# Four attention layers on one core: which exponentials VectorE takes over, chosen while the work is laid out instead of by a fixed table

## The chip, the cores and the metric

The kernel runs on one core of one Trainium2 chip. The metric is the time of one execution in microseconds on the device. Three executions of the kernel before took 2187.83, 2191.64 and 2196.76 us, a median of 2191.64 us. A further execution was taken by the profiler, and all rows below come from it.

The engines are named as in the profile: PE (TensorE, matrix products; PEld its weight loads), ACT (ScalarE, here nearly only exponentials), DVE (VectorE, elementwise work), POOL (GpSimd, masks and the issuing of some transfers), SP (SyncE, the issuing of the other transfers). SBUF is the on-chip memory, PSUM the accumulator that PE writes, eight banks of 512 numbers in each of 128 partitions.

## The reference

Two attention blocks A and B with their own weights are applied in turn, A, B, A, B, each to the layer-normed residual stream. S = 2048 tokens, D = 640, 32 heads of 20 numbers. A looks back over a window of 256 tokens, B looks at all tokens.

```python
qkv = (x @ wqkv).reshape(B, S, 3, H, Dh)...          # q, k, v per head
scores = jnp.einsum("bhqd,bhkd->bhqk", q, k) * (Dh ** -0.5)
# A only: scores = where(0 <= i - j < 256, scores, -1e9)
p = softmax(scores, axis=-1)
o = jnp.einsum("bhqk,bhkd->bhqd", p, v)
return o.reshape(B, S, D) @ wo

x = x + A(layernorm(x)); x = x + B(layernorm(x))
x = x + A(layernorm(x)); x = x + B(layernorm(x))
```

In B every one of 32 heads has 2048 x 2048 scores, and each of them goes through an exponential. That is the bulk of the work.

## The kernel before

Layers are numbered 0 to 3; 0 and 2 are windowed (A), 1 and 3 are full (B). Queries are cut into four chunks c of 512, heads into eight groups g of four. A *unit* is a layer, a chunk and a head group; in layers 1 and 3 chunk 0 is further cut by keys into parts, so that it can start before all keys exist. A full unit has 16 blocks of 128 keys times 4 heads, 64 *banks* of scores (128 keys by 512 queries each, one PSUM bank). The list `units` fixes their order: chunk 0 of layer 0, then the rest of layer 0 with three parts of layer 1's chunk 0 between, then layer 1 from chunk 1 with layer 2 woven in after some of its head groups, then layer 3.

**The main loop** takes one *tile* of scores per turn: three banks (two in every second turn of the early units, and a fourth now and then in layer 3's last chunks), which stand in one half of PSUM, banks 0 to 2 and 3 to 5 in turn. PE writes the scores, ACT takes the exponential of the whole tile in one instruction into an SBUF tile `pt` (line 1387), and two or three turns later PE multiplies values by it (line 1420) and accumulates the unit's output in PSUM bank 7. After a unit's last block `finish_unit` copies that bank out with DVE. Everything is written out in program order; each engine runs its own instructions in that order, and semaphores hold it where data or a buffer is missing.

**Background work** (layer norms, projections, output projections, the division by the row sums in `t_tail`) is a set of Python generators. In each turn `background` pumps some of them, with a credit set by `rate` from how much work is due before which unit. They use PSUM banks 5 and 6, one after the other, and DVE empties those banks (`evac`, lines 307 to 331). `keep_clock` adds matmuls of constants (`masks,ident`) where PE would otherwise have less to do than a set amount.

**Banks aside.** Some banks are not given to ACT. DVE computes their exponential in fp16 bit arithmetic, two banks (a *pair*) at a time. The scores of each bank are converted to fixed point (line 957), then follows a chain of four steps on the pair of 1024 columns: the fraction (line 969), its square (978), a cubic (980), and the sum with the whole part (982). The result is multiplied with the values by two matmuls of line 1010. The pair needs an input buffer `xi`, a shared scratch `t` and an output buffer `out`. In layer 1 these live in the space of `raw_o` (two inputs, three outputs), in layer 3 in idle transposed-input tiles and idle key and query tiles (two inputs, five outputs), set up by `side_early` and `side_start`.

Which banks these are is a fixed table: `put_aside` gives each full unit from chunk 1 on the last blocks of its keys, 4 banks in layer 1 and 8 or 6 in turn in layer 3, with none in layer 3's first chunk (nor in chunk 1's first head group). All tiles up to layer 3's chunk 1 are put together before the loop starts: in layer 1 a bank aside stands as the third bank of a tile (ACT then takes only two) at every fifth tile of the unit. In layer 3 from chunk 1 on the bank goes to PSUM bank 6 beside a full tile, when `side_free` finds a loaded unit, a free bank and a free input.

**The planner's backlog** `state["lag"]` estimates how far DVE is behind, in us: each DVE instruction adds a set cost, each turn takes off the time that ACT needs for its tile. The chain is advanced by `side_work` at the end of a turn:

```python
while (force or state["lag"] < WORK) and side["chain"]:   # WORK = 1.0
    cost = next(side["chain"][0], None)
```

At a unit's last block `side_done` forces whatever of its pairs is still missing.

The functions around the change follow with the line numbers of the profile.

Of the kernel before, what the change touches and what calls it, by code (L numbers as in the profile page):

```python
# [23 lines left out]
NT = S // P  # L24
# [16 lines left out]
WORK = 1.0  # L41
SIDE_1 = 4
SIDE_3 = (6, 8)
# [9 lines left out]
def kernel(  # L53
# [629 lines left out]
    def put_aside(l, c, g):  # L683

        if l == 1:
            n = SIDE_1
        else:
            n = 4 if (c, g) == (NC - 1, G - 1) else SIDE_3[g % 2]
        if n == 2:
            return ((NT - 1, 2), (NT - 1, 3))  # L690
        return tuple((NT - 1 - i // 4, i % 4) for i in range(n))

# [3 lines left out]
    class Unit:  # L696
        def __init__(self, l, c, g, part=None):
            self.l, self.c, self.g, self.part = l, c, g, part
            self.windowed = l % 2 == 0
            self.aside = ()  # L700
            if self.windowed:
                sets = [(m, b0, subs, j) for m, b0, subs in window_banks(c) for j in range(4)]
            else:

                if c > 0 and (l, c, g) != (3, 1, 0):
                    self.aside = put_aside(l, c, g)
                k0, k1 = key_blocks(l, part)
                sets = [
                    (None, 0, [(kc, 0, 4, 0)], j) for kc in range(k0, k1) for j in range(4)
                    if (kc, j) not in self.aside  # L710
                ]
            n = len(sets)
            self.banks = [
                (self, j, m, b0, subs, i < 4, i >= n - 4 + len(self.aside), i == n - 1)
                for i, (m, b0, subs, j) in enumerate(sets)
            ]
# [144 lines left out]
    def finish_unit(u):  # L861
# [31 lines left out]
    side_todo = deque(  # L893
        (u, p, i) for u in units for p in range(len(u.aside) // 2) for i in range(2)
    )
    side_left = Counter({id(u): len(u.aside) for u in units})
    side_out = {}
    side = {"xi": deque(), "chain": deque(), "out": deque(), "late": False}
# [7 lines left out]
    def side_start():  # L906

        assert live["xnT"] == 0 and not side["chain"] 
# [28 lines left out]
    def side_scores():  # L937

        u, p, i = side_todo[0]
        mseq[0] += 1  # L940
        mfree[6] = (state["tick"] + 2, mseq[0])
        kc, j = u.aside[2 * p + i]
        z = ps[:, 6, :]
        nc.tensor.matmul(z, lhsT=u.k(kc, j), rhs=u.q(j, 0, 4), start=True, stop=True)  # L944
        side_fixed(z)

    def side_fixed(z):

        u, p, i = side_todo.popleft()
        side_left[id(u)] -= 1  # L950
        if not side_left[id(u)] and id(u) in deferred:
            live["kt"] -= 1
            live["qt"] -= 1
        if i == 0:
            side["now"] = side["xi"].popleft()
        xi = side["now"]
        nc.vector.tensor_scalar(  # L957
# [4 lines left out]
        if i == 1:  # L962
            side["chain"].append(t_chain(u, xi))

    def t_chain(u, xi):
# [3 lines left out]
        V.tensor_scalar(  # L969
            out=t, in0=xi.bitcast(I16)[:, 0::2], scalar1=T1, scalar2=T0, op0=ALU.mult, op1=ALU.add  # L970
        )
        yield 0.7
        while not side["out"]:
            yield 0.0
        pt = side["out"].popleft()
        po = pt.rearrange("p a b -> p (a b)")
        q = po.bitcast(F16)
        V.tensor_tensor(out=q, in0=t, in1=t, op=ALU.mult)  # L978
        yield 0.7
        V.scalar_tensor_tensor(out=q, in0=q, scalar=TB, in1=t, op0=ALU.add, op1=ALU.mult)  # L980
        yield 1.2
        V.scalar_tensor_tensor(
            out=po.bitcast(U16), in0=xi.bitcast(I32), scalar=1.0 / C, in1=q,
            op0=ALU.mult, op1=ALU.add,
        )
        side["xi"].append(xi)
        side_out.setdefault(id(u), []).append((pt, state["tick"]))
        yield 1.2

    def side_work(force):  # L990

        while (force or state["lag"] < WORK) and side["chain"]:
            cost = next(side["chain"][0], None)
            if cost is None:
                side["chain"].popleft()
                continue
            if cost == 0.0:
                return False
# [5 lines left out]
    def side_values(u, pairs, done):  # L1004

        for n in range(done, len(pairs)):
            pt = pairs[n][0]
            for i in range(2):
                kc, j = u.aside[2 * n + i]
                nc.tensor.matmul(  # L1010
                    op[32 * j : 32 * j + VW, :], lhsT=u.v(kc, j), rhs=pt[:, i, :], start=False,
                    stop=all(jj != j for _, jj in u.aside[2 * n + i + 1 :]),
                    skip_group_check=True,
                )
            side["out"].append(pt)

    def side_push():
# [3 lines left out]
        if side_free():  # L1021
            side_scores()
# [7 lines left out]
    def side_done(u):  # L1030

        n = 0
        while len(side_out.get(id(u), ())) < len(u.aside) // 2:
            n += 1
            assert n < 10000
            side_push()
        return side_out.pop(id(u))
# [5 lines left out]

    def s_emitted(u):
# [6 lines left out]
        elif side_left[id(u)]:  # L1051
# [187 lines left out]
    with tc.manual_schedule():  # L1239
# [11 lines left out]
        banks = [b for u in units for b in u.banks]  # L1251
        tiles = []
        starts = {}
        n = 0
        last_layer = sum(len(u.banks) for u in units[: index[3, 1, 0, None]])
        placed = {}
        while n < last_layer:
            size = 2 if len(tiles) % 2 and narrow(banks[n][0]) else 3
            u = banks[n][0]
            at = placed.setdefault(id(u), [])  # L1260
            extra = []
            if (
                len(at) < len(u.aside) and banks[n + 1][0] is u
                and len(tiles) >= (15 // (SIDE_1 - 1) if SIDE_1 > 2 else 3) * len(at) + (at or [0])[0]
            ):
                kc, j = u.aside[len(at)]
                extra = [(u, j, "side", 0, [(kc, 0, 4, 0)], False, False, False)]
                at.append(len(tiles))
                size = 2
            for b in banks[n : n + size]:  # L1270
                starts.setdefault(id(b[0]), len(tiles))
            tiles.append(banks[n : n + size] + extra)
            n += size
        for m, b in enumerate(banks[n:]):
            starts.setdefault(id(b[0]), len(tiles) + m // 3)
        banks = deque(banks[n:])

        side_now = False

        def next_tile(t):  # L1280

            if t < len(tiles):
                return tiles[t]
            size = 3
            if side_now:
                return [banks.popleft() for _ in range(min(size, len(banks)))]
# [236 lines left out]
```

## Time and profile before

| | before |
|---|---|
| median of three executions | 2191.64 us |
| lowest, highest | 2187.83, 2196.76 us |
| profiled execution, its own time | 2197.81 us |
| its span, first to last instruction | 2196.1 us |
| ACT busy | 2112.9 us (96%) |
| PE busy | 1931.1 us (88%) |
| DVE busy | 1324.3 us (60%) |
| POOL busy | 483.3 us (22%) |
| granted PE clock, mean | 0.993 |

The page also gives the busy share in 40 equal slices of the span (one slice is 54.9 us), a digit for tenths. The groups name a line of the kernel, engine, operation, what it writes and reads, how many there were, the busy time, the mean length of one, and the engine's idle time just before them with what ended it. In the tables of stretches each engine has its busy time and, in brackets, its number of instructions. Records of consecutive ACT instructions overlap a little, so sums of lengths can pass the length of a stretch.

### The profile page before, as it was taken

The numbers are of one execution on the slowest core, as the hardware profiler recorded it, in microseconds if no ns is written. First come the engines' busy times: TensorE is split into PE (matmuls) and PEld (weight loads), VectorE is DVE, ScalarE is ACT, GpSimd is POOL, SyncE is SP. The second block draws the span as 40 slices with busy tenths as digits, with TensorE's granted clock in tenths as the row PEclk, the third lists the DMA queues.
The fourth block names the chain that finished last, engine by engine and source line by source line (L and its number), as shares of the span: only waits on it lengthen the run. The fifth ranks groups of instructions, "written<-read, shape, count | busy, mean of one in ns | idle before, by whom it ended". The sixth has DMA issues, their size and how long they took to land. (4 is left out here: it accounts for less than half of the span.)

```text
span 2196.1 us, 73000 instructions
## 1 busy us (share of the span) xinstructions
PE 1931.1 (88%) x31782; PEld 760.4 (35%) x31783; DVE 1324.3 (60%) x2308; ACT 2112.9 (96%) x1726; POOL 483.3 (22%) x952
## 2 busy tenths in 40 slices
PE   8999998988889888888888988888888988888887
PEld 3444443433333333333333433342222222222222
DVE  5556565425656666566665743532487778778873
ACT  7789899999999999999999999999999999999997
POOL 6665556110121113401143112511000000000000
PEclk9899999999999999999999999999999999999999
DMA  6223233322210323112231123122112111111100
GB/s 201 74 82 107 68 98 99 81 78 64 74 46 27 83 60 90 39 37 64 64 101 34 35 86 98 39 57 65 48 43 61 32 32 41 35 32 35 53 20 17
DMA packets 88416, 137.27 MB, mean 63 GB/s; under 512 B 20766, under 2 KB 63486, under 8 KB 88094
## 3 DMA queue, kind: packets, MB, share of 16 engines
q1 hardware_dynamic: 68878, 79.43, 13.1%
q0 software_dynamic: 19216, 53.17, 8.2%
q8 instruction: 249, 4.08, 0.8%
q14 instruction: 73, 0.60, 0.1%
HBM read 99.52 MB, written 27.79 MB: 58 GB/s over the span
## 5 line engine op out<-in xcount | busy, mean ns | idle before, releaser
L1387 ACT ACTIVATE pt<-ps 128x1536 bf16<-128x1536 f32 (+2 forms) x1646 | 2072.1, 1438 | 46.1 <-PE ps L1359 36.1
L1359 PE MATMUL ps<-qt,kt 32*128 32x512 bf16 x3938 | 542.4, 384 | 79.3 <-ACT pt L1387 70.2
L307 PE MATMUL ps<-masks,ident 128*32 128x512 bf16 x5676 | 504.6, 387 | 99.4 <-ACT pt L1387 54.8
L1420 PE MATMUL ps<-pt,vt 128*21 128x512 bf16 x3826 | 383.1, 387 | 1.1 <-issue 1.1
L1359 PEld LDWEIGHTS <-kt 32*128 32x128 bf16 x3938 | 161.0, 91 | 482.7 <-issue 461.0
L307 PEld LDWEIGHTS <-ident 128*32 128x32 bf16 x5676 | 179.9, 94 | 283.1 <-issue 254.7
L1463 POOL TENSOR_SCALAR_AFFINE_SELECT pt<-pt 128x256 bf16<-128x256 bf16 (+2 forms) x505 | 213.2, 444 | 184.4 <-ACT pt L1387 181.8
L307 PE MATMUL ps<-xnT,wqk 128*32 128x512 bf16 x3320 | 224.8, 381 | 12.4 <-DVE on L1128 2.8
L331 DVE CAST st<-ps 128x512 bf16<-128x512 f32 x134 | 92.7, 691 | 169.1 <-PE ps L307 164.9
L1420 PEld LDWEIGHTS <-vt 128*21 128x21 bf16 x3842 | 95.0, 89 | 254.9 <-issue 251.5
L957 DVE TENSOR_SCALAR xnT<-ps 128x512 int32<-128x512 f32 x158 | 109.2, 691 | 109.2 <-PE ps L944 108.4
L307 PE MATMUL ps<-wop,on 128*32 128x320 bf16 x3712 | 160.9, 300 | 6.8 <-DVE x_sb L579 3.3
L1474 DVE TENSOR_TENSOR pt<-pt,masks 128x512 bf16<-128x512 bf16 (+4 forms) x267 | 111.3, 433 | 61.3 <-ACT pt L1387 59.8
L307 PEld LDWEIGHTS <-on 128*32 128x32 bf16 x5760 | 122.2, 95 | 66.6 <-issue 33.6
L1359 PE MATMUL ps<-qa,ka 32*128 32x384 bf16 (+2 forms) x1408 | 114.5, 278 | 24.4 <-ACT pt L1387 21.2
L307 PE MATMUL ps<-wv,xnT 128*32 128x320 bf16 x2560 | 116.6, 302 | 7.9 <-DVE on L1128 3.3
L579 DVE TENSOR_TENSOR x_sb<-x_sb,ps 128x320 bf16<-128x320 bf16 x120 | 58.3, 486 | 105.8 <-PE ps L307 104.9
L307 PEld LDWEIGHTS <-wqk 128*32 128x32 bf16 x3320 | 83.5, 96 | 95.9 <-issue 38.0
L1128 DVE TENSOR_TENSOR on<-on,ps 128x512 bf16<-128x512 bf16 x128 | 86.3, 683 | 47.8 <-PE ps L307 46.9
L885 DVE CAST on<-ps 128x512 bf16<-128x512 f32 x112 | 77.1, 688 | 61.7 <-PE ps L1010 36.1
L957 DVE TENSOR_SCALAR raw_o<-ps 128x512 int32<-128x512 f32 x96 | 66.1, 689 | 61.4 <-PE ps L1359 60.3
L546 POOL DMA_DIRECT2D k_d<-st x75 | 42.6, 568 | 224.2 <-DVE st L331 209.1
(101 smaller groups left out, 1638.5 us busy)
## 6 DMA issues: line engine op xcount, KB each, us to landing
vt<-v_d SPq DMA_DIRECT2D x48, 336.0 KB
kt<-k_d SPq DMA_DIRECT2D x192, 80.0 KB
wqk<-in_B_wqkv_dram POOLq DMA_DIRECT2D x80, 160.0 KB, 3.5
wqk<-in_A_wqkv_dram POOLq DMA_DIRECT2D x70, 160.0 KB, 3.5
k_d<-st POOLq DMA_DIRECT2D x75, 128.0 KB, 2.3
q_d<-st POOLq DMA_DIRECT2D x75, 128.0 KB, 2.1
qt<-q_d SPq DMA_DIRECT2D x384, 20.0 KB
v_d<-vs POOLq DMA_DIRECT2D x16, 336.0 KB, 3.1
```

The costliest lines, as they stand in the source:

```text
L307: nc.tensor.matmul(out_[r], lhsT=lhsT[:, r], rhs=rhs, start=start, stop=stop)
L331: nc.vector.tensor_copy(out=out_, in_=in_)
L546: nc.gpsimd.dma_start(out=dst, in_=staging.pop())
L579: nc.vector.tensor_tensor(out=xv, in0=had, in1=yp, op=ALU.add)
L885: nc.vector.tensor_copy(out=oT, in_=op)
L957: nc.vector.tensor_scalar(out=xi.bitcast(I32)[:, i * C : (i + 1) * C], in0=z, scalar1=SCALE * LOG2E * FIX, scalar2=127.5 * FIX, op0=ALU.mu ...
L1128: nc.vector.tensor_tensor(out=oT, in0=oT, in1=zb, op=ALU.mult)
L1359: nc.tensor.matmul(sp[:, i, col * P : (col + qn) * P], lhsT=u.k(kc, j), rhs=u.q(j, q0, qn), start=True, stop=True,)
L1387: nc.scalar.activation(out=pt[:, i:k, b0 * P :], in_=sp[:, i:k, b0 * P :], func=ACT.Exp, scale=SCALE,)
L1420: nc.tensor.matmul(op[32 * j : 32 * j + VW, q0 * P : (q0 + qn) * P], lhsT=u.v(kc, j), rhs=pg[:, i, col * P : (col + qn) * P], start=(first ...
L1463: nc.gpsimd.affine_select(out=v, in_=v, compare_op=ALU.is_gt if later else ALU.is_ge, fill=0.0, base=0, pattern=[[0, k - i], [-1 if later ...
L1474: nc.vector.tensor_tensor(out=pt_[:, i:k, cols], in0=pt_[:, i:k, cols], in1=mv_, op=ALU.mult)
```

## The change

The table `put_aside`, the tile list that was made ahead, and the counters that went with them are gone. Each unit now keeps a queue `rest` of its banks, and tiles are taken from it turn by turn. In every turn, while the backlog is under 0.5, `side_giver` looks for a unit, the current one or one of the next two, that is loaded and has enough banks left (30, or 12 when nothing has been taken from it by a tile), and `side_take` takes two banks from the end of its queue as the next pair.

Up to layer 3's chunk 1 a bank aside is still the third bank of a three-bank tile, and until `side_start` has run two of them are at least five turns apart (`GAP_1`). `side_start` now runs in layer 3's chunk 0, from its fifth head group on, as soon as at most one transposed-input tile is in use, so that this chunk gives banks too. From chunk 1 on the bank goes to PSUM bank 6 as before. A chain step is now issued only if the backlog with the step's own cost stays under 1.7 (`WORK_1`, until `side_start`) or 2.2 (`WORK`, from then on). A pair's values are multiplied as soon as the pair has been done for three turns. Some of the planner's costs change, and `rate` works from fractions of units instead of numbers of tiles.

In the built program VectorE has 300 banks instead of 254. The numbers of transfers on SP are the same, 1481.

```diff
 LAG = 0.5
-WORK = 1.0
-SIDE_1 = 4
-SIDE_3 = (6, 8)
+LAG_1 = 0.5
+WORK = 2.2
+WORK_1 = 1.7
+KEEP = 30
+HALF = False
+MOST_1 = 64
+GAP_1 = 5
...
-            state["lag"] += 0.6
+            state["lag"] += 0.7 if in_.shape[-1] == C else 0.5
...
-        state["lag"] += 1.2
+        state["lag"] += 1.1
...
+        def pop(self):
+            if self.windowed:
+                return self.rest.popleft()
+            kc, j = self.rest.popleft()
+            end = not self.rest
+            return (self, j, None, 0, [(kc, 0, 4, 0)], kc == self.k0, end, end)
...
-    def side_free():
-        if not side_todo or not side["late"]:
-            return False
-        u, p, i = side_todo[0]
-        return (
-            id(u) in loaded and state["tick"] >= loaded[id(u)] + 8
-            and mfree[6][0] <= state["tick"] and (i == 1 or len(side["xi"]) > 0)
-        )
+    def side_giver():
+        if not side["late"] and state["tick"] < side["last"] + GAP_1:
+            return None
+        if side["half"] is not None:
+            return side["half"][0]
+        if not side["xi"]:
+            return None
+        while side["at"] < len(givers) and not givers[side["at"]].rest:
+            side["at"] += 1
+        for n in range(side["at"], min(side["at"] + 3, len(givers))):
+            u = givers[n]
+            if id(u) not in loaded or state["tick"] < loaded[id(u)] + 8:
+                return None
+            if not side["late" if u.l == 3 else "early"]:
+                return None
+            if u.l == 1 and len(u.aside) >= MOST_1:
+                continue
+            if len(u.rest) >= (KEEP if len(u.rest) + len(u.aside) < u.size else 12):
+                side["at"] = n
+                return u
+        return None
+
+    def side_take(u):
+        if side["half"] is not None:
+            return side["half"][1]
+        j = u.rest.pop()
+        i = u.rest.pop()
+        u.aside += (i, j)
+        side["half"] = (u, i, j)
+        return i
...
     def side_work(force):
-        while (force or state["lag"] < WORK) and side["chain"]:
-            cost = next(side["chain"][0], None)
...
+        while side["chain"]:
+            step, h, cost = side["chain"][0][0]
+            if step.__name__ == "square" and not side["out"]:
+                return False
+            if not force and state["lag"] + cost > (WORK if side["late"] else WORK_1):
+                return False
...
+        def next_tile(t, giver):
+            if state["unit"] < final:
+                size = 2 if t % 2 and narrow(flow[0]) else 3
+                if giver is None or size == 2:
+                    return take(size)
+                kc, j = side_take(giver)
+                return take(2) + [(giver, j, "side", 0, [(kc, 0, 4, 0)], False, False, False)]
...
-                if t >= len(tiles) and not side["late"] and not live["xnT"] and not todo:
+                if (
+                    not side["late"] and state["unit"] >= index[3, 0, 4, PARTS[3][0]]
+                    and live["xnT"] <= 1 and not live["qa"] and not live["ka"]
+                ):
                     side_start()
-                side_now = (
-                    state["held"] is None and state["lag"] < LAG and side_free()
-                )
-                cur = next_tile(t)
+                giver = side_giver() if state["lag"] < (LAG if side["late"] else LAG_1) else None
+                if giver is not None and state["unit"] >= final and (
+                    state["held"] is not None or mfree[6][0] > state["tick"]
+                ):
+                    giver = None
+                cur = next_tile(t, giver)
```

`final` is the first unit of layer 3's chunk 1. The steps of the chain are the same four, now kept as a list of functions instead of a generator (`HALF` is off, so they stay undivided).

More of the change, by code (lines that the diff above doesn't have):

```diff
@@ L891 @@
     ended_units = []
-    side_todo = deque(
-        (u, p, i) for u in units for p in range(len(u.aside) // 2) for i in range(2)
-    )
-    side_left = Counter({id(u): len(u.aside) for u in units})
     side_out = {}
-    side = {"xi": deque(), "chain": deque(), "out": deque(), "late": False}
+    side = {
+        "xi": deque(), "chain": deque(), "out": deque(), "late": False, "early": False,
+        "half": None, "at": 0, "last": 0,
+    }
+    givers = [u for u in units if not u.windowed and (u.l, u.c) != (1, 0)]
     def side_tiles(xi, t, outs):
@@ L906, in side_start @@
     def side_start():
-        assert live["xnT"] == 0 and not side["chain"]
+        assert live["xnT"] <= 2 and not side["chain"] and side["half"] is None
         tl = [xtp.tile([P, KD, C], BF16, name="xnT", tag="xnT") for _ in range(3)]
@@ new lines, in chain @@
+        every = (slice(0, 2 * C),)
+        halves = (slice(0, C), slice(C, 2 * C)) if HALF and u.l == 1 else every
+        cost = 0.7 if len(halves) == 2 else 1.25
+        steps = [(fraction, h, 0.7) for h in every] + [(square, h, 0.7) for h in every]
+        steps += [(cubic, h, cost) for h in halves] + [(whole, h, cost) for h in halves]
+        return deque(steps)
+    def side_work(force):
+        while side["chain"]:
[4 more added lines that the diff above has]
+                return False
+            side["chain"][0].popleft()
+            if not side["chain"][0]:
@@ L995, in side_work @@
                 side["chain"].popleft()
-                continue
-            if cost == 0.0:
-                return False
+            step(h)
             state["lag"] += cost
@@ L1020, in side_push @@
             return
-        if side_free():
-            side_scores()
+        if side["half"] is not None and mfree[6][0] <= state["tick"]:
+            side_scores(side["half"][0])
             return
@@ L1050, in s_emitted @@
                 ka_free.append(ka.pop((c, u.g)))
-        elif side_left[id(u)]:
+        elif side["half"] is not None and side["half"][0] is u:
             deferred.add(id(u))
@@ L1249 @@
         woven = index[1, 0, 0, PARTS[1][0]]
[L1251 to L1273, printed above, removed]
@@ new lines, in take @@
+        def take(count):
+            got = []
+            while flow and len(got) < count:
+                got.append(flow[0].pop())
+                if not flow[0].rest:
+                    flow.popleft()
+            return got
+        def next_tile(t, giver):
[5 more added lines that the diff above has]
+                return take(2) + [(giver, j, "side", 0, [(kc, 0, 4, 0)], False, False, False)]
```

191 lines of the change are left out of this document (92 added, 99 removed).

## The prediction

> **What bounds the kernel now.** I read the page first, its engine shares and the row of forty slices, then the table of stretches, then ScalarE's groups by form inside each stretch.
>
> ```profile
> span 2196.1 us, 73000 instructions
> DVE  5556565425656666566665743532487778778873
> ACT  7789899999999999999999999999999999999997
> L1387 ACT ACTIVATE pt<-ps 128x1536 bf16<-128x1536 f32 (+2 forms) x1646 | 2072.1, 1438 | 46.1 <-PE ps L1359 36.1
> ```
> ScalarE is at nine tenths or more from the fifth slice to the last but one, and nearly all of it is the exponential of line 1387. So an exp bank (512 scores per partition) that leaves ScalarE is worth something in every later slice; VectorE has 3 to 5 tenths left in most of them.
>
> The stretches below are, in order: layer 1 from chunk 1 with layer 2 woven in (VectorE's early banks); layer 3 chunk 0 up to its fourth head group, with layer 2's last chunk; the rest of that chunk 0; and layer 3's chunks 1 to 3 (the late banks).
>
> ```profile
> 498.60:1285.60 787.00, 688.19 (x11543) 281.88 (x11535) 493.11 (x867) 774.29 (x626) 173.11 (x324) 1.00 0.22 59
> 1285.60:1415.60 130.00, 112.73 (x2005) 47.46 (x2005) 53.86 (x115) 128.93 (x97) 48.03 (x96) 1.00 0.26 72
> 1415.60:1559.80 144.20, 123.07 (x2006) 49.96 (x1999) 41.59 (x86) 143.92 (x108) 18.38 (x28) 0.99 0.22 61
> 1559.80:2196.10 636.30, 558.77 (x7400) 175.76 (x7400) 466.68 (x621) 620.41 (x459) 0.00 (x0) 0.99 0.12 36
> ```
> The columns after the length are PE, weight loads, VectorE, ScalarE, GpSimd. VectorE is 63%, 41%, 29% and 73% busy; the third stretch has the most room.
>
> Records of consecutive exps overlap, so their mean length overstates what one costs. Thirty-four of the three-bank form in a row, from the timeline of ScalarE:
>
> ```profile
> 1371.49 45.89 ACT L1387 ACTIVATE pt<-ps 128x1536 bf16<-128x1536 f32 x34
> ```
> Without the last one's own length (about 1.7 us) that is 44.2 / 33 = 1.339 us each. ScalarE's groups by form, of the four stretches (the last one up to 2183 us):
>
> ```profile
> L1387 ACT ACTIVATE pt<-ps 128x1536 bf16<-128x1536 f32 x486 | 673.5, 1534 | 12.0 <-PE ps L1359 11.0
> L1387 ACT ACTIVATE pt<-ps 128x1024 bf16<-128x1024 f32 x104 | 115.1, 1114 | 0.1
> L1387 ACT ACTIVATE pt<-ps 128x768 bf16<-128x768 f32 x16 | 13.7, 896 | 0.5 <-issue 0.4
> L1387 ACT ACTIVATE pt<-ps 128x1152 bf16<-128x1152 f32 x4 | 5.2, 1301 | 0.0
> L1387 ACT ACTIVATE pt<-ps 128x256 bf16<-128x256 f32 x8 | 3.8, 474 | 0.2
> L1387 ACT ACTIVATE pt<-ps 128x512 bf16<-128x512 f32 x4 | 2.7, 673 | 0.0
> L1387 ACT ACTIVATE pt<-ps 128x384 bf16<-128x384 f32 x4 | 2.6, 648 | 0.0
> ...
> L1387 ACT ACTIVATE pt<-ps 128x1536 bf16<-128x1536 f32 x97 | 130.7, 1638 | 1.1 <-PE ps L1359 1.1
> ...
> L1387 ACT ACTIVATE pt<-ps 128x1536 bf16<-128x1536 f32 x108 | 145.7, 1724 | 0.3 <-PE ps L1359 0.3
> ...
> L1387 ACT ACTIVATE pt<-ps 128x1536 bf16<-128x1536 f32 x454 | 614.9, 1520 | 4.1 <-PE ps L1359 2.3
> L1387 ACT ACTIVATE ka<-ps 128x2048 bf16<-128x2048 f32 x4 | 8.1, 2034 | 0.0
> ```
> One bank is 1534 - 1114 = 0.42 us of ScalarE. At 1.339 us for three banks and 0.42 less per bank the first stretch needs 486 x 1.339 + 104 x 0.92 + 16 x 0.71 + 4 x 1.02 + 8 x 0.28 + 4 x 0.50 + 4 x 0.39 = 768 us and takes 787: 19 us lost. The second needs 129.9 of 130.0 and the third 144.6 of 144.2: nothing lost. Chunks 1 to 3 need 454 x 1.339 + 4 x 1.78 = 615 of 623.4: 8 us lost. Loss shows only where VectorE takes banks: 19 us over 96 early banks is 0.20 us a bank, 8 us over 158 late ones 0.05. A bank aside therefore gains 0.42 and gives back 0.20 or 0.05. The timeline shows such a loss beside an early bank:
>
> ```profile
> 1086.60 1.22 DVE L982 SCALAR_TENSOR_TENSOR raw_o<-raw_o 128x1024 uint16<-128x1024 int32 x1
> 1087.74 0.68 DVE L957 TENSOR_SCALAR raw_o<-ps 128x512 int32<-128x512 f32 x1
> 1088.34 0.68 DVE L1128 TENSOR_TENSOR on<-on,ps 128x512 bf16<-128x512 bf16 x1
> 1089.07 0.86 PE L307 MATMUL ps<-wv,xnT 128*32 128x320 bf16 x20 [0.86 <-DVE on L1128]
> 1089.87 0.39 PE L1359 MATMUL ps<-qt,kt 32*128 32x512 bf16 x3
> 1090.36 2.91 ACT L1387 ACTIVATE pt<-ps 128x1536 bf16<-128x1536 f32 x2 [0.92 <-PE ps L1359]
> ```
> A chain step, then the bank's conversion, then the tail's product on VectorE; PE waits for the bank that the product frees, the next scores stand behind it in PE's order, and ScalarE idles 0.92 us.
>
> **The change part by part.** The order of instructions in the two built programs gives the counts. VectorE's banks go from 254 to 300: layer 1 from 96 to 110, layer 3 chunk 0 from 0 to 24, chunk 1 from 50 to 54, chunk 2 unchanged at 56, chunk 3 from 52 to 56. ScalarE has 37 fewer three-bank exps and 33 more two-bank ones. The DMA queues keep their 1481 transfers on SP and, but for one mask more, POOL its list; PE gets 6 more idle-filling groups of four matmuls. VectorE gets 23 chains:
>
> ```profile
> L957 DVE TENSOR_SCALAR raw_o<-ps 128x512 int32<-128x512 f32 x96 | 66.1, 689 | 61.4 <-PE ps L1359 60.3
> L982 DVE SCALAR_TENSOR_TENSOR raw_o<-raw_o 128x1024 uint16<-128x1024 int32 x48 | 58.6, 1221 | 0.9
> L980 DVE SCALAR_TENSOR_TENSOR raw_o<-raw_o 128x1024 f16<-128x1024 f16 x48 | 58.5, 1220 | 0.9
> L969 DVE TENSOR_SCALAR raw_o<-raw_o 128x1024 f16<-128x1024 int16 x48 | 33.2, 691 | 0.8
> L978 DVE TENSOR_TENSOR raw_o<-raw_o 128x1024 f16<-128x1024 f16 x48 | 32.9, 686 | 0.8
> ```
> A pair costs 2 x 0.69 + 1.22 + 1.22 + 0.69 + 0.69 = 5.2 us, so 23 pairs are 120 us: +36 in the first stretch (67% busy), +62 in the third (72%), +21 in chunks 1 to 3 (77%). None of them passes the 73% to 77% at which the late banks run now with little loss, which is the cover; gone, it would show as PE waiting for VectorE.
>
> 1. Fourteen banks more in layers 1 and 2: 14 x (0.42 - 0.20) = 3.1 us gained; ends 0 (loss equals gain) and 5.9 (no loss).
> 2. Twenty-four in chunk 0, all in the third stretch, as the third bank of score tiles with projections still on PE. Nothing of before shows banks aside there. The nearest row is the early bank, same form of tile: 24 x (0.42 - 0.20) = 5.3 us; at the late price 24 x 0.37 = 8.9, at no loss 10.1, and at the early price doubled 0.5.
> 3. Eight in chunks 1 to 3, in PSUM's spare bank: 8 x 0.37 = 3.0 us.
> 4. The choice by backlog. A bank is now taken only while the planner's backlog is under 0.5 us, and a chain step only while backlog plus step stays under 1.7 us (early), where before a step could start at 1.0 and end at 2.2. In the two orders the projections and tails that PE runs between a side tile and the next fall from 10.6 matmuls a tile (mean of 96) to 8.2 (of 110). Scaled so, 0.20 becomes 0.155, on 134 tiles 6 us; since the backlog is a plan and not the real queue I take half, 3.0; ends -5 (choice worse than the fixed places) and 15 (early banks at the late price).
> 5. Closing a head group. Three groups close with the last chain step, 1.22 us, not yet issued: VectorE does it then, the pair's values wait behind it on PE, and behind those the next scores, while ScalarE lives on the tile ahead. I count 0.6 us each, 1.8 lost; ends 0 and 3.7.
>
> Moving the late work tiles 107 tiles ahead takes three of five transposed-input buffers while one or none is in use: nothing is late by that, since only one projection chunk is left.
>
> Sum: 3.1 + 5.3 + 3.0 + 3.0 - 1.8 = 12.6 us. The profiled execution took 2197.81 us (2196.1 span, 1.7 around it), 0.28% over the median 2191.64; 2185.2 there is 2179.0 at the median's level.
>
> **The rivals.**
> *The loss eats the gain.* The third stretch gets 19 of its 24 in 64 tiles, beside 718 matmuls of projections; if a bank there and in layer 1 costs 0.40 instead of 0.20, terms 1 and 2 fall to 0.8 and term 4 to nothing: 3.0 + 0.8 - 1.8 = 2 us, 2190. For it speaks the 0.92 us above; against it that VectorE stands free there for 29% of work only.
> *Loss nearly vanishes.* If the gate keeps VectorE's queue short at every side tile, all early banks cost 0.05: 46 x 0.37 + 96 x 0.15 = 31 us, 2160. Against it: the plan's backlog at a side tile was at or under 0.45 us in nine of ten cases before, too.
> *Slower: chains beside the masks.* Sixteen of the new program's early banks fall into layer 2's tiles, where GpSimd masks.
>
> ```profile
> sum 79.10, PE 67.64 PEld 28.98 DVE 49.50 ACT 77.96 POOL 51.38; mean PE 16.91 PEld 7.24 DVE 12.38 ACT 19.49 POOL 12.84
> ...
> ACT pt L1387 <- POOL pt L1463: 3.0, 2, 2.5
> ```
> In its four stretches between 607 and 934 us GpSimd is 65% busy, with 27.7 us spare. If the three longest kinds of chain step (0.69 + 1.22 + 1.22) each held a mask up for their whole length, 8 pairs make 25 us; masks late hold the values, their buffers and then the exps. It decides once over 12.6 of the 25 us come through; in full it gives 2197.8 + 12.4, at the median's level 2204. Against it, ScalarE waited for masks twice in the whole run. [...]
> That the change does not do what it says is out: the counts above are in the program.
>
> **How the numbers follow.** Forecast (2171 to 2187) 0.52, loss eats gain 0.25, loss vanishes 0.12, masks 0.11. The range 2165 to 2195 leaves out half of the vanishing case and most of the masks. 0.5%, about what a measurement of this kernel tells from no change, is 11 us: faster (under 2180.7) takes the vanishing case and 0.36 of the forecast's 0.52, 0.48; slower the masks and a little, 0.12; same 0.40. Both signs do not hold much, so one range stands.
>
> **What would show it.** Right: the third stretch, now 144.2 us, comes at about 139 with some 104 us of VectorE in it; chunks 1 to 3 shorter by 3; layer 1 and 2 by 5 or so; VectorE busy near 1444 us; ScalarE's idle time before exps no more than 46.1. Wrong: many PE waits for VectorE's conversions and evacuations ahead of the scores in the third stretch, GpSimd ahead of exps in layer 2, or a chunk 0 as long as before.

## The result

The changed kernel takes 2181.89 us (median of 15 executions, 2180.22 to 2186.74), the kernel before 2192.97 us beside it (15 executions). The ratio is 0.9955, 95% interval 0.9946 to 0.9964: 9.9 us less, 7.9 to 11.8 (the two medians lie 11.1 us apart). The forecast was 2179.0 us, 12.6 us less, in a range of 2165 to 2195. By its time, the case held likeliest is the one that came; whether it came for the reasons given is looked at below.

The page of the changed kernel:

```profile
span 2180.2 us, 73213 instructions
DVE  6656564425666666766667633576688778777876
ACT  7899899999999999999999999999999999999998
L1429 ACT ACTIVATE pt<-ps 128x1536 bf16<-128x1536 f32 (+2 forms) x1641 | 2054.5, 1415 | 53.2 <-PE ps L1405 35.4
```

The exponential is now line 1429, the scores line 1405, the values line 1462, the values of banks aside line 1055, the last chain step line 1015. ScalarE is as full as before with 18 us less work in it. VectorE has more in the middle and at the end. The same four stretches, cut where the units begin (lengths, then PE, weight loads, VectorE, ScalarE, GpSimd):

```profile
493.30:1278.70 785.40, 693.78 (x11583) 282.99 (x11583) 528.08 (x909) 768.03 (x623) 180.01 (x324) 1.00 0.22 60
1278.70:1407.90 129.20, 112.74 (x1989) 47.17 (x1982) 53.03 (x115) 129.18 (x98) 47.37 (x93) 1.00 0.28 74
1407.90:1549.50 141.60, 123.92 (x2001) 48.74 (x2001) 97.22 (x158) 135.50 (x108) 19.59 (x31) 1.00 0.24 62
1549.50:2180.20 630.70, 555.69 (x7417) 173.28 (x7409) 487.62 (x647) 617.35 (x457) 0.00 (x0) 1.00 0.13 36
```

Cut the same way, the kernel before has 787.0, 130.1, 144.2 and 637.6 us. So layers 1 and 2 give 1.6 us, the two parts of chunk 0 give 0.9 and 2.6, chunks 1 to 3 with the tail 6.9, of which the tail (what follows the last exponential) 1.2. That is 12.0 of the 15.9 us between the two profiled spans. The other 3.9 us lie ahead of layer 1's chunk 1, where no bank is aside in either kernel; the section on the hardware looks at 3.5 of them. The profiled execution of the kernel before took 2197.81 us, more than any of the 15 beside it, so that differences between these two profiles are larger than the gain of 9.9 us.

ScalarE's waits in layers 1 and 2 hold one that the kernel before does not have there:

```profile
ACT pt L1429 <- PE ps L1405: 11.0, 25, 1.4
ACT pt L1429 <- PE ps L1462: 3.8, 2, 2.4
ACT pt L1429 <- POOL pt L1500: 0.8, 2, 0.5
```

An exp waits for the values matmuls because these still hold the six score tiles `pt`. The timeline of the longest one:

```profile
1254.65 0.38 PE L1055 MATMUL ps<-raw_o,vt 128*21 128x512 bf16 x2
1254.69 1.23 DVE L1015 SCALAR_TENSOR_TENSOR raw_o<-raw_o 128x1024 uint16<-128x1024 int32 x1
1255.97 0.39 PE L1055 MATMUL ps<-raw_o,vt 128*21 128x512 bf16 x2 [0.94 <-DVE raw_o L1015]
1256.39 0.69 DVE L883 CAST on<-ps 128x512 bf16<-128x512 f32 x1 [0.48 <-PE ps L1055]
1258.67 0.61 PE L1462 MATMUL ps<-pt,vt 128*21 128x512 bf16 x8
1259.16 1.45 ACT L1429 ACTIVATE pt<-ps 128x1536 bf16<-128x1536 f32 x1 [2.43 <-PE ps L1462]
```

A *closing* is the end of a head group, where the values of its last pairs must be multiplied. This is one of the three closings that force a chain step: the step of 1.23 us is issued only now, PE stands 0.94 us before it, the closing is five tiles late, the next group's values come at 1258.67, and ScalarE has stood 2.43 us without a free tile.

### The profile page after: what moved, and what is told of

It reads as the page before. It is cut to its first block, busy times and chain, and to the rows that moved or that the text cites. A ratio compares the mean times of both kernels' runs of the same rounds, so it can differ in the third digit from the quotient of the medians.

```text
span 2180.2 us, 73213 instructions
## 1 busy us (share of the span) xinstructions
PE 1931.5 (89%) x31807; PEld 755.9 (35%) x31807; DVE 1434.5 (66%) x2447; ACT 2094.8 (96%) x1721; POOL 490.9 (23%) x953
## 4 chain that ended last, share of the span: by engine, by line
ACT 49%; PE 25%; issue 15%; DVE 8%; POOL 1%; DMA 1%; ACTq 0%; DVEq 0%; POOLq 0%
ACT pt L1429 48%; PE ps L311 14%; PE ps L1405 6%; PE ps L1462 3%; DVE on L1175 1%; POOL pt L1500 1%; DVE pt L1511 1%; DVE st L335 1%; DMA wqk<-in_B_wqkv_dram 1%; DVE x_sb L583 0%; PE ps L964 0%; PE ps L451 0%; DVE xnT L981 0%; DVE ka L1009 0%; DMA wqk<-in_A_wqkv_dram 0%
## 5 line engine op out<-in xcount | busy, mean ns | idle before, releaser
L1429 ACT ACTIVATE pt<-ps 128x1536 bf16<-128x1536 f32 (+2 forms) x1641 | 2054.5, 1415 | 53.2 <-PE ps L1405 35.4
L1405 PE MATMUL ps<-qt,kt 32*128 32x512 bf16 x3930 | 548.1, 384 | 64.8 <-ACT pt L1429 57.0
L1462 PE MATMUL ps<-pt,vt 128*21 128x512 bf16 x3780 | 377.4, 386 | 1.5 <-issue 1.0
L1405 PEld LDWEIGHTS <-kt 32*128 32x128 bf16 x3930 | 156.2, 91 | 468.2 <-issue 449.3
L1500 POOL TENSOR_SCALAR_AFFINE_SELECT pt<-pt 128x256 bf16<-128x256 bf16 (+2 forms) x506 | 220.9, 458 | 191.7 <-ACT pt L1429 179.0
L981 DVE TENSOR_SCALAR xnT<-ps 128x512 int32<-128x512 f32 x190 | 131.0, 690 | 113.9 <-PE ps L964 108.0
L1462 PEld LDWEIGHTS <-vt 128*21 128x21 bf16 x3796 | 93.6, 89 | 254.5 <-issue 251.0
L981 DVE TENSOR_SCALAR raw_o<-ps 128x512 int32<-128x512 f32 x110 | 75.6, 688 | 37.1 <-PE ps L1405 34.5
```

The costliest lines, as they stand in the source:

```text
L981: nc.vector.tensor_scalar(out=xi.bitcast(I32)[:, i * C : (i + 1) * C], in0=z, scalar1=SCALE * LOG2E * FIX, scalar2=127.5 * FIX, op0=ALU.mu ...
L1405: nc.tensor.matmul(sp[:, i, col * P : (col + qn) * P], lhsT=u.k(kc, j), rhs=u.q(j, q0, qn), start=True, stop=True,)
L1429: nc.scalar.activation(out=pt[:, i:k, b0 * P :], in_=sp[:, i:k, b0 * P :], func=ACT.Exp, scale=SCALE,)
L1462: nc.tensor.matmul(op[32 * j : 32 * j + VW, q0 * P : (q0 + qn) * P], lhsT=u.v(kc, j), rhs=pg[:, i, col * P : (col + qn) * P], start=(first ...
L1500: nc.gpsimd.affine_select(out=v, in_=v, compare_op=ALU.is_gt if later else ALU.is_ge, fill=0.0, base=0, pattern=[[0, k - i], [-1 if later ...
```

## The experiments

All are edits of the changed kernel. "Loss" is the length of the stretch of layers 1 and 2 less what ScalarE needs at its clean rate, worked out as in the prediction: 768 us with 96 banks aside there and 0.42 less for each further one. By that the kernel before loses 19 us there, the changed one 785.4 - 762.1 = 23. Some of the expectations count with the shortest distances between two exponentials, 1.33 and 0.90 us instead of 1.339 and 0.92. By that count every loss is some 10 us higher (33 us for the changed kernel), and differences between kernels stay as they are.

**Closing without a forced step.**

```diff
+HURRY = 0
-            if not force and state["lag"] + cost > (WORK if side["late"] else WORK_1):
+            if not force and (len(side["owner"][0].rest) > HURRY or side["owner"][0].l == 3) and state["lag"] + cost > (...):
```

> Edit: a chain step is issued whatever the backlog once the head group it belongs to has no scores left to give; 302 banks aside instead of 300, no head group closes with a chain step missing (three did). Theory A (closings that hold PE behind a chain step are a main part of the loss in layers 1 and 2): those three cost 2.8, 1.7 and 0.75 us in the trace of the changed kernel, so the stretch of layers 1 and 2 comes at about 780 instead of 785 us and the whole 4 to 6 us under the changed kernel. Theory B (they only take idle time that the background work would take otherwise): within 1.5 us of the changed kernel.

Measured 2185.27 us, 0.9974 (0.9964 to 0.9985). The stretch takes 789.5 us, 4 more than in the changed kernel, though no closing there is forced or over three tiles late. But PE's waits for the last chain step are not gone, they have grown: 5.8 us in four waits instead of 3.0 in three. So this edit only moved the waits and does not decide between the theories; the run with 42 banks left, below, does.

**No banks in chunk 0.**

```diff
-                    not side["late"] and state["unit"] >= index[3, 0, 4, PARTS[3][0]]
+                    not side["late"] and state["unit"] >= final
```

> Edit: the late work tiles are set up only at layer 3's chunk 1, so that chunk 0 gives no bank; 276 banks aside, the early and the late ones as in the changed kernel. By the prediction (a bank there at the price of an early one, 0.20 us) the time is 5.3 us over the changed kernel. By the trace of the changed kernel (that stretch 144.2 to 141.6 us) it is 2.6 us over. If the loss there eats the gain, 0.

Measured 2183.89 us, 0.997 (0.9958 to 0.9982). In its trace layers 1 and 2 are the same to 0.1 us, and the third stretch is 2.2 us longer than with the 24 banks:

```profile
1408.70:1552.50 143.80, 123.19 (x2029) 49.90 (x2029) 41.96 (x87) 143.79 (x109) 19.25 (x31) 1.00 0.23 61
```

The gain there is 2.2 to 2.6 us of 10.1 that ScalarE saves, a loss of about 0.3 us a bank instead of the 0.20 assumed. The 2.2 is the better figure: in the kernel before, PE ran 3.4 us of this stretch at half clock (see the section on the hardware), in the other two none.

**Four banks a head group.**

```diff
-MOST_1 = 64
+MOST_1 = 4
```

> Edit: at most four banks aside in a head group of layer 1, 96 as before the change, still placed by the gate; one head group closes with a step missing instead of three. By the prediction (14 banks, 0.22 us each) 3.1 us over the changed kernel. If the closings are what costs, two of them less give 2 to 4 us back, and the time is within 1.5 us of the changed kernel or under it.

Measured 2191.83 us, 1.0001 (0.9993 to 1.001): 8 to 10 us over the changed kernel, more than either theory gave. The stretch:

```profile
495.80:1287.50 791.70, 688.98 (x11661) 280.83 (x11657) 489.19 (x865) 773.19 (x623) 173.69 (x319) 1.00 0.21 57
```

It is 6.3 us longer, but a stall that is not at a bank aside stands at its very end:

```profile
1279.63 1.26 PE L311 MATMUL ps<-xnT,wqk 128*32 128x512 bf16 x20 [0.60 <-DVE vs L335]
1281.93 0.56 POOL L550 DMA_DIRECT2D k_d<-st  x1 [1.05 <-DVE st L335]
1286.83 0.60 PE L1405 MATMUL ps<-qt,kt 32*128 32x512 bf16 x1 [5.61 <-DMA kt<-k_d]
1287.53 1.45 ACT L1429 ACTIVATE pt<-ps 128x1536 bf16<-128x1536 f32 x1 [7.45 <-PE ps L1405]
```

In this kernel's order the product for keys comes just before layer 3's first scores. The keys are written out (`k_d`) and read back (`kt`), PE waits 5.61 us for them, and ScalarE 7.45. The changed kernel has no such wait there. Less these 7.45 us the stretch is 784.2 us, 1.2 less than with 110 banks. By this estimate, from one profile, 96 banks at the gate's places lose 16 us, against 19 at the fixed table's, and the 14 banks more gain nothing: they save 5.9 us and lose 7. Two of the three forced closings come with them. Nearly all the rest of this kernel's longer span lies in the 2.5 us ahead of the stretch, where its instructions are those of the changed kernel, and in the first part of chunk 0, right behind the stall (132.7 us against 129.2).

**The chain left out.**

```diff
-    # fraction, square and cubic: bodies removed
-            V.scalar_tensor_tensor(out=q.bitcast(U16)[:, h], in0=xi.bitcast(I32)[:, h], scalar=1.0 / C, in1=q[:, h], ...)
+            V.tensor_scalar(out=q.bitcast(U16)[:, h], in0=xi.bitcast(I32)[:, h], scalar1=1.0 / C, scalar2=0.0, ...)
```

> Edit: the fraction, square and cubic steps of every chain are left out and the last step reads the fixed-point scores alone, so that the exponential of the 300 banks aside is not computed; order, tiles and banks unchanged. VectorE's work for a pair falls from 5.2 to about 2.3 us. If the loss at banks aside is VectorE's queue (evacuations and closings behind chain steps), nearly all of it goes: layers 1 and 2 fall from 785 to about 762 us and the whole by 25 to 35 us. If it is PE, which cannot fill the next tile within the 0.9 us of a two-bank exp, it stays but for the closings: the whole falls by 5 to 8 us.

Measured 2173.54 us, 0.992 (0.9906 to 0.9934): 8 to 10 us under the changed kernel. The first and the third stretch:

```profile
493.00:1277.60 784.60, 696.44 (x11583) 285.25 (x11583) 364.50 (x744) 767.26 (x624) 173.38 (x324) 0.99 0.22 60
1406.70:1545.70 139.00, 124.00 (x2005) 48.81 (x2001) 64.97 (x123) 134.85 (x109) 20.14 (x31) 1.00 0.23 63
```

VectorE loses 164 of its 528 us in layers 1 and 2, and the stretch 0.8. The 0.8 is too small: the profile is of the longest of the six executions, and it has a stall of its own at a closing, where PE waits 1.14 us for weights and ScalarE 4.16. By the medians the whole kernel gains 8 to 10 us, where all of the loss in layers 1 and 2 and in chunk 0 is some 30 us. So most of the loss is not VectorE's queue, and the gain is near what the second theory gave.

**The changed kernel again**, without an edit.

> The changed kernel itself, beside the next three on one chip, so that they can be compared with it and not only with the kernel before. Both theories: 0.995 to 0.997 of the kernel before.

Measured 2183.40 us, 0.9966 (0.9954 to 0.9979). The changed kernel is thus between 0.9955 and 0.9966 in the comparisons here.

**No bank aside in layer 1.**

```diff
-MOST_1 = 64
+MOST_1 = 0
```

> Edit: no bank aside in layer 1 (110 fewer); layer 3 as in the changed kernel. Theory P (the prediction's: a loss per bank aside, 0.2 to 0.3 us): layers 1 and 2 run at ScalarE's clean rate, so the 33 us lost there fall to under 8 and the stretch grows by 110 x 0.42 - 25 = 21 us. Theory Q (the loss is background work of PE and buffers, whatever is aside; shown by the kernel with 96 banks there, which lost as much as the one with 110): it stays above 20 us and the stretch grows by 33 us or more.

Measured 2205.91 us, 1.0068 (1.0052 to 1.0084).

```profile
490.10:1301.20 811.10, 686.34 (x11625) 288.93 (x11621) 258.72 (x578) 809.17 (x626) 172.70 (x323) 1.00 0.22 57
```

The stretch needs 768 + 96 x 0.42 = 808.3 us and takes 811.1: 3 us lost. With no bank aside ScalarE runs close to its clean rate, and 110 banks shorten the stretch by 25.7 us, 0.23 us each of the 0.42 saved. Theory P had 21 us, theory Q 33 or more; P is nearer, though by the count of its own expectation 12 us stay lost instead of under 8. A bank costs 0.17 us at the old places ((19 - 3) / 96) and 0.19 at the new ((23 - 3) / 110; 0.18 in the second profile of the changed kernel, where the stretch takes 784.8 us).

**Banks three tiles apart.**

```diff
-GAP_1 = 5
+GAP_1 = 3
```

> Edit: early banks may stand three tiles apart instead of five; 130 early banks instead of 110, six closings with a chain step missing instead of three. Theory P: 20 x 0.1 to 0.2 = 2 to 4 us gained, less 3 x 1.7 us for the closings: from 2 us slower to 2 us faster than the changed kernel. Theory Q: 20 x 0.42 = 8 us gained less the closings, 3 us or more faster.

Measured 2203.68 us, 1.0056 (1.004 to 1.0073): 20 us slower than the changed kernel, outside both theories. The stretch and ScalarE's waits in it:

```profile
493.80:1300.30 806.50, 698.31 (x11579) 283.10 (x11579) 576.74 (x970) 763.73 (x625) 184.40 (x325) 0.99 0.21 58
...
ACT pt L1429 <- PE ps L1405: 22.8, 48, 2.8
ACT pt L1429 <- PE ps L1462: 16.4, 9, 5.9
```

With 130 banks the loss is 53 us. Of the 30 us more, 12.6 are waits for score tiles, as in the closing shown above; six closings are forced and eight are five tiles late.

**Less of PE's background at side tiles.**

```diff
-            r = rate(t)
+            r = rate(t) * (n_b / 3 if side["last"] == state["tick"] and state["unit"] < final else 1)
```

> Edit: in a turn whose tile gives a bank aside, PE's background credit is cut to two thirds, as its idle-filling already is; 302 banks. If the loss beside side tiles is PE, which has the background work of a full turn to do in the 0.9 us of a two-bank exp, the excess right behind side tiles (19 us in the first three tiles each in layers 1 and 2, 8 in chunk 0) falls by a third or more: 6 to 9 us faster than the changed kernel. If the work only moves to the next tile and holds that up, within 2 us.

Measured 2188.54 us, 0.9986 (0.9974 to 0.9998): 4 to 7 us slower than the changed kernel; layers 1 and 2 take 790.1 us. This does not show what the background costs at side tiles, because the edit moved the closings too: in the profile PE waits 2.96 us for a last chain step at two of them, and ScalarE 3.29 and 6.62 us behind these.

**Closing after four tiles.**

```diff
-                if end and u.aside and pts and not side_ready(u) and group[-1][0] > t - 5:
+                if end and u.aside and pts and not side_ready(u) and group[-1][0] > t - 4:
```

> Edit: the last values of a head group wait at most four tiles for its pairs instead of five; 300 banks, same places, the same three forced closings; no closing five tiles late (five were). If ScalarE's new waits for the values matmuls are score buffers held by late closings (6.0 us in four waits in the changed kernel, 0 before), most of them go: 2 to 4 us faster than the changed kernel. If they belong to the forced chain step itself, they only move to the scores: within 1 us.

Measured 2182.13 us, 0.9951 (0.9938 to 0.9964): no difference from the changed kernel. In layers 1 and 2, which take 788.8 us in the profile:

```profile
ACT pt L1429 <- PE ps L1405: 16.6, 30, 2.9
...
ACT pt L1429 <- PE ps L1462: 0.2, 1, 0.2
```

The waits for score tiles are gone, 3.8 to 0.2 us, and the waits for scores have grown by 5.6: the forced step is now waited for there.

**Banks only while 42 are left.**

```diff
-KEEP = 30
+KEEP = 42
```

> Edit: a head group gives banks only while 42 are left in it instead of 30, so that its pairs are done earlier; 302 banks, none of the closings forced and in layers 1 and 2 none five tiles late. If the closings are 5 us of loss, layers 1 and 2 come at about 780 us and the whole 4 to 6 us under the changed kernel. If the loss is only in how PE's background meets the side tiles, within 2 us, either way.

Measured 2182.20 us, 0.9954 (0.994 to 0.9969). No closing is forced, the stretch takes 785.7 us, and the loss stays at 24 us. The 5.3 us that the three forced closings cost in the trace came back elsewhere, in layer 1's chunk 1 above all (251.0 us against 248.7, from its first exponential to chunk 2's).

**Denser, with early closings.**

```diff
-KEEP = 30
-WORK_1 = 1.7
-GAP_1 = 5
+KEEP = 46
+WORK_1 = 2.0
+GAP_1 = 4
```

> Edit: early banks four tiles apart, 46 left, chain bound 2.0 instead of 1.7; 134 early banks (130 with three apart) but no closing forced and none over three tiles late. If the jump of the loss at 130 banks (from 33 to 63 us) is its closings, this kernel keeps a loss of about 40 us: layers 1 and 2 at about 782 us and the whole 2 to 5 us faster than the changed kernel. If it is the density of side tiles, the loss is 50 us or more: 8 us or more slower.

Measured 2184.56 us, 0.996 (0.9944 to 0.9976).

```profile
494.50:1280.60 786.10, 702.28 (x11645) 282.11 (x11642) 582.85 (x983) 762.81 (x624) 181.67 (x327) 1.00 0.22 60
```

134 banks lose 34 us, where 130 with late closings lost 53. So the jump with three tiles between goes with its closings for the larger part, although the spacing differs too, four tiles against three. But against 110 banks the 24 more save 10 us and lose 11: at this density a further bank gains nothing.

**No gate on the backlog.**

```diff
-LAG_1 = 0.5
+LAG_1 = 99.0
```

> Edit: no bound on the planner's backlog for taking an early bank; 302 banks, the spacing of five tiles and the bounds of the chain steps stay. If the choice by backlog is worth what the prediction gave it (3 us), 3 us slower than the changed kernel. If the spacing alone sets the places (112 early banks against 110), within 1.5 us.

Measured 2195.04 us, 1.0011 (1.0 to 1.0021): 10 to 12 us slower than the changed kernel, with all but the same banks (112). The planner's order shows only 8 of the 112 taken at a backlog of 0.5 or more, one of them at 4.5. The trace shows one closing that costs most, with neither of its two pairs done:

```profile
1259.92 1.21 DVE L1009 SCALAR_TENSOR_TENSOR raw_o<-raw_o 128x1024 f16<-128x1024 f16 x1
1261.16 1.22 DVE L1015 SCALAR_TENSOR_TENSOR raw_o<-raw_o 128x1024 uint16<-128x1024 int32 x1
1262.31 0.68 DVE L997 TENSOR_SCALAR raw_o<-raw_o 128x1024 f16<-128x1024 int16 x1
...
1265.01 1.23 DVE L1015 SCALAR_TENSOR_TENSOR raw_o<-raw_o 128x1024 uint16<-128x1024 int32 x1
...
1266.29 0.60 PE L1055 MATMUL ps<-raw_o,vt 128*21 128x512 bf16 x2 [3.46 <-DVE raw_o L1015]
...
1270.01 2.37 ACT L1429 ACTIVATE pt<-ps 128x1024 bf16<-128x1024 f32 x2 [7.35 <-PE ps L1462]
```

Six chain steps stand one behind the other, PE waits 1.34 and 3.46 us for them, and ScalarE 7.35, where the longest wait of an exponential in the changed kernel is 2.43. The stretch of layers 1 and 2 is 8.8 us longer (794.2), and this closing is the larger part. The gate is worth 10 us in this kernel, by the few banks that it refuses.

Of all these only the kernel without the chain, which does not compute the exponentials aside, is faster than the changed kernel beyond its interval.

## Why the prediction was right, point by point

- **The bound and the price of a bank.** ScalarE's work set the time. The clean rate was read from two stretches without banks aside, and the kernel with none in layer 1 confirms it where they had been: 3 us lost in 811 (12 by the shortest distances between exponentials). The price of 0.20 us read from 19 us over 96 banks was 0.17 to 0.19.
- **Terms 1, 4 and 5, layers 1 and 2** (3.1 gained by 14 banks, 3.0 by the choice, 1.8 lost at closings: 4.3 in sum). Measured 1.6 (2.2 in the second profile). The step that failed is term 1, that a further bank costs what the average one did: with 96 banks at the gate's places the stretch is 784.2 us without its stall, with 110 it is 785.4 and 784.8, so that the 14 banks gave nothing. Term 4 is not refuted: 787.0 - 784.2 = 2.8 us for the gate's places at the same number of banks, near its 3.0, but this is an estimate from one profile, and no run separates the reason given (fewer matmuls behind a side tile). Against choosing by spacing alone the gate counts for 10 us. The closings of term 5 were named rightly and were undersized: 2.8, 1.7 and 0.75 us by the distances between exponentials, 5.3 in place of 1.8. Taking them out gave nothing back, so that they are not simply a cost on top.
- **Term 2, chunk 0** (5.3): 2.2 to 2.6. The price at the stretch was 0.3 instead of 0.20; VectorE's use came as forecast, 97 us against 104.
- **Term 3, chunks 1 to 3** (3.0): 5.7 without the tail. Chunk 1 gives 3.7, chunk 3 3.2, chunk 2 loses 1.2. Eight banks save ScalarE only 3.4 us, so something else is in it. It is not that the work tiles are set up earlier: the kernel without banks in chunk 0 sets them up at chunk 1 again and takes 209.0 us there, against 208.8 in the changed kernel and 212.5 before. The profile of the kernel before has a piece at half clock there (1562.2 to 1565.6 us), with 0.75 us lost at one exponential, and the other two have none. The rest stays open.
- **The sum** was 12.6, the runs say 9.9. That they lie so near is luck in part. Terms 1, 2, 4 and 5 were to give 9.6 us and gave about 4; the late chunks gave nearly twice their 3.0, for reasons that are open in part.
- **The rivals.** The loss took about half of the gain at the new banks, not all: where the first rival has terms 1, 2, 4 and 5 at -1.0 us and the forecast at 9.6, the 4 lie half way. In layers 1 and 2 alone, where the 14 banks gave nothing, that rival was right. The loss did not vanish. Chains beside masks cost little: the masks took 220.9 us (506 of them) instead of 213.2 (505), while ScalarE's waits for them went from 3.0 to 3.5 us in the whole run. No run shows that a chain step holds a mask up for its whole length as a rule, which the third rival took for its 25 us. Of the four masks in the trace of the changed kernel that start beside a chain step of its two longest kinds (1.22 us in the mean), three take 1.19, 1.24 and 1.50 us, where the medians of their sizes are 0.29, 0.41 and 0.52, and one takes 0.40 at a median of 0.29. The first of the three ends 0.15 us after the step:

```profile
931.45 1.22 DVE L1015 SCALAR_TENSOR_TENSOR raw_o<-raw_o 128x1024 uint16<-128x1024 int32 x1
931.63 1.19 POOL L1500 TENSOR_SCALAR_AFFINE_SELECT pt<-pt 128x128 bf16<-128x128 bf16 x1 [0.82 <-ACT pt L1429]
```

- **The signs.** The third stretch came at 141.6 us instead of 139 and VectorE at 1434.5 us busy instead of 1444. One sign came out the other way: ScalarE's idle time before exponentials was to be no more than 46.1 us and is 53.2, the closings among it.

What the 20 us of loss in layers 1 and 2 consist of stays open in part. It is not the chains' time on VectorE for the most part, since leaving three of four steps out gained 8 to 10 us in the whole kernel. It rises with the number of two-bank tiles, and PE is 87% to 89% busy there, 85% with no bank aside. That PE, with the same work in fewer microseconds, has too little slack to fill each next tile in time fits these numbers; it is argued and not shown, and the run that cut PE's background at side tiles moved the closings too and cannot tell.

## What to carry to other kernels

Read the price of moving work off a full engine from a stretch that has such work and one that has none, and expect the price to rise with density: here 0.42 us saved left 0.23 on average for the first 110 banks, nothing for the last 14 of them by the estimate above, and nothing for the next 24. When work is done ahead on a second engine, its deadline can matter more than its load: here one closing whose pairs were not done cost ScalarE 7 us, more than the choice of places gained. A gate that refuses few cases can be worth much, and its value is seen by taking it out and not by counting what it refuses. And before two stretches are compared, look at their ends: one late load of keys hid there what the 14 banks were worth.

## What the runs showed of the hardware

In the profiles of the kernel before and of the changed kernel the clock granted to PE is full or half, nothing between. The kernel before has six pieces of 3.4 us at half clock and one of 10.2, the changed kernel four of 3.4 and one of 6.8; in each the end of the execution cuts off one more. Part of what differs between the two profiles goes with these pieces. The kernel before took 67.8 us from the first exponential to that of layer 0's second chunk, and the changed one 64.3, although PE, VectorE and ScalarE have the same instructions in the same order in both up to 148 us. The stretches from 50.0 us on, first of the kernel before, then of the changed kernel (the third column from the end is the granted clock):

```profile
50.00:53.40 3.40, 1.22 (x37) 0.60 (x37) 0.95 (x2) 1.82 (x3) 3.37 (x7) 1.00 0.74 191
53.60:56.90 3.30, 3.30 (x66) 1.82 (x62) 0.86 (x2) 2.14 (x3) 0.40 (x1) 0.50 0.25 63
```

```profile
50.00:53.40 3.40, 3.31 (x101) 1.89 (x97) 1.87 (x5) 3.40 (x7) 3.11 (x7) 1.00 0.45 126
53.60:56.90 3.30, 2.13 (x51) 0.92 (x42) 0.65 (x4) 1.94 (x5) 0.00 (x0) 1.00 0.14 45
```

In the kernel before PE was busy for 1.22 of 3.4 us, and the next piece was at half clock; in the changed kernel it was busy for 3.31, and the clock stayed full. With the same instructions in both, the 3.5 us between 67.8 and 64.3, nearly all of the 3.9 us ahead of layer 1's chunk 1, are no gain of the change. All the edited kernels have the changed kernel's instructions up to that chunk, and in their profiles it begins anywhere from 488.8 to 497.2 us.

Half clock also came after a piece with more work in it, in the changed kernel:

```profile
877.90:881.30 3.40, 2.13 (x31) 0.85 (x25) 3.40 (x9) 3.14 (x3) 2.99 (x7) 1.00 0.16 36
881.50:884.70 3.20, 3.20 (x39) 1.16 (x43) 1.23 (x3) 1.72 (x2) 0.49 (x1) 0.50 0.16 47
```

Here PE was busy for 2.13 us (63%) of the 3.4 us before, and its longest wait in them was 1.27 us. From 557.1 to 560.5 us of the same profile PE was busy for 2.11 us (62%), and the clock stayed full, so that by these two pieces the busy share alone does not tell when it falls. At the closing of 7.35 us in the kernel without the gate 10.2 us at half clock follow on 3.4 us in which PE was busy for 0.89:

```profile
1260.60:1264.00 3.40, 0.89 (x9) 0.20 (x7) 3.30 (x5) 1.99 (x2) 2.79 (x4) 1.00 0.85 223
1264.10:1274.30 10.20, 7.52 (x87) 2.12 (x90) 4.21 (x7) 3.81 (x3) 0.00 (x0) 0.50 0.40 108
```

In the kernel with four banks a head group the stretch right behind the stall of 7.45 us took 132.7 us, against 129.2 in the changed kernel. Whether a lower clock is behind this was not shown.

Where the clock is only full or half, the mean clock of an execution gives its time at half clock, (1 - clock) x 2 x span. For the kernels without early banks and without the gate, and for the executions without a profile, this is an estimate that takes their clocks to be so too. The mean clocks of four profiles:

```profile
core 0: 2196.1 us, clock 0.993
```

```profile
core 0: 2180.2 us, clock 0.995
```

```profile
core 0: 2202.6 us, clock 0.997
```

```profile
core 0: 2195.3 us, clock 0.992
```

These are the kernels before and after, the one without early banks, and the one without the gate: 31, 22, 13 and 35 us at half clock. Among the 15 executions of the changed kernel the three shortest (2180.2 to 2180.3 us) had 0.996 and the three longest (2185.2 to 2186.7) 0.992 to 0.994; between them the order is loose (2180.9 us with 0.993). By these clocks the longest had 9 to 17 us more at half clock, three to five pieces, for some 5 to 6 us. A difference of 5 us between two profiles of this kernel can thus go with a few such pieces; that they are its cause was not shown.
